# The q projection of two chunks as one Strassen pair, and a ring of weight sums at another place

## The chip, the cores and the metric

The kernel runs on one core of one Trainium2 chip. The core has five engines with instruction queues of their own: TensorE (PE in the profile, its weight loads PEld), VectorE (DVE), ScalarE (ACT), GpSimd (POOL) and SyncE (SP), which here only issues transfers. They work at the same time and meet at semaphores. The metric is the device time of one execution in microseconds; less is better. Before the change it is 770.33 us, the median of three runs (770.24 to 770.73).

## The reference

One transformer block over 2048 rows of 1024 values, in bfloat16. Its attention has 32 heads of 32 values and looks at eight earlier rows, two apart.

```python
qkv = (layernorm(x) @ wqkv)                      # 1024 -> 3 * 1024
idx = pos[:, None] - (jnp.arange(8) * 2)[None, :]
logits = einsum("bhsd,bhswd->bhsw", q, k[:, :, idx]) * 32 ** -0.5   # masked where idx < 0
o = einsum("bhsw,bhswd->bhsd", softmax(logits), v[:, :, idx])
h = x + o.reshape(B, S, D) @ wo
n = layernorm(h)
out = h + ((n @ w_gate) * (n @ w_up)) @ w_down   # 1024 -> 3584 -> 1024
```

## The kernel before, in words

The 2048 rows are four chunks (0 to 3) of 512. A chunk goes through normalization, q, k and v projection, attention, output projection `wo` with the residual, a second normalization, gate and up projections, their product, and the down projection.

**TensorE.** A product of a 128-column block of weights with a chunk is a group of eight 128x128 by 128x512 matmuls (`mm_group`, L431), each group into one of eight PSUM buffers. ScalarE copies most of them out (`evac_qkv`, L344; L717 and L724 for chunk 0's gate and up, L766 for chunk 1's). The weights stream through `wpool`, seven buffers of 1 MB (tag "w"): `pump` loads the next when fewer than seven are live, `retire` gives one back. wqkv has six blocks of 512 columns: 0 and 1 give q, 2 and 3 k, 4 and 5 v. One group is 1.73 us (`GROUP_US`).

**The order.** Each engine executes its instructions in the order in which the program issues them (`manual_schedule`). The order at the end of the function reads, for chunk and blocks: `qkv(0, 1..3)`, `qkv(1, 0..3)`, `qkv(0, 4..5)`, `qkv(1, 4..5)`, `qkv(2, 0..5)`, `qkv(3, 0..3)`, output projection 0 (`wo_ln2`), `qkv(3, 4..5)`, `ffn1_first` (gate and up of chunk 0, with output projection 1 in its middle, `wo_1`), `ffn1_second` (gate and up of chunk 1), `wo_adds(2)` (output projection 2). Then come the down projection of chunks 0 and 1 (lines `ex`, `ev`, `ey`, `ez`), output projection 3 in its middle, the gate and up projections of chunks 2 and 3 (`pair_block`), and their down projection (`dx`, `dy`). These last three are already computed by Strassen's scheme: seven products in place of eight over 2x2 blocks, with sums of blocks ahead and sums of results behind.

**Background work.** Attention of a chunk runs on VectorE: eight multiplications of 4096 elements per partition for the scores and eight for the values, with adds between, some 84 us a chunk. It is a Python generator. `Background` issues a piece of it after each group: `step` adds the group's time times `rate` to a credit of at most 4 us, and pieces are issued as long as the credit is positive, each taking the estimate that it yields. Other VectorE work is taken off with `spend`. A piece that yields `("later", us)` waits so long in the program's own count of time. So credit decides where in each queue an attention piece stands; it does not know how far an engine really is. Chunk 3's attention is cut off from the background at `wo_adds(2)`; its remaining pieces are issued by hand there and in the down projection (`pull`). The exp of each attention is on ScalarE (L499), the subtraction ahead of it (L497) on VectorE. An attention ends with its store and the loads of `oT` by GpSimd (L536, L539), which the output projection of the chunk needs.

**Sums for the scales.** The Strassen parts run in float16. Their weights are scaled by a power of two from the sum of absolute values. `Scale.add` sums one tile on ScalarE (L635), `rows` adds the columns up on VectorE (L639, L640), and `total` sums over the partitions by a product with ones on TensorE (L645), followed by five tiny VectorE steps (L647 to L654). For the down weights `abs_down` streams one half (columns 512 to 1023) in seven pieces through one `wpool` buffer, the ring, two pieces in flight; the other half is summed by `abs_blocks` at the start of `wo_adds(2)`, sixteen ScalarE passes (`junkb`). `scale_d.rows()` and `scale_d.total()` stand in the first products of the down projection.

Of the kernel before, what the change touches and what calls it, by code (L numbers as in the profile page):

```python
# [78 lines left out]
def kernel(  # L79
# [46 lines left out]


# [72 lines left out]
    def load_x(c, what, eng):  # L200
        tiles = []
        for t in range(4):
            xt = hp.tile([128, D], BF, tag="h", name=f"{what}{c}_{t}")
            eng.dma_start(xt[:], x[bass.ds(c * TC + t * 128, 128), :])
            tiles.append(xt)
        return tiles
# [52 lines left out]
    class NormOnScalar(Norm1):  # L259
# [16 lines left out]
        def devs(self):  # L276
            nc.scalar.activation(self.nm, self.s, ACTF.Copy, scale=-1.0 / D)
            for t in range(4):
                nc.scalar.activation(self.junk[:], self.xs[t][:], ACTF.Square, bias=self.nm[:, t:t + 1],
                                     accum_out=self.ss[:, t:t + 1])  # L280
                yield "later", self.pace
            nc.scalar.activation(self.rs4[:], self.ss, ACTF.Ln, bias=eps[:], scale=1.0 / D)
            nc.scalar.activation(self.rs4[:], self.rs4[:], ACTF.Exp, scale=-0.5)
            for t in range(4):
                nc.scalar.activation(self.nb[:, t:t + 1], self.nm[:, t:t + 1], ACTF.Copy, scale=self.rs4[:, t:t + 1])
# [14 lines left out]
        def rows(self):  # L300
            for t in range(4):
                self.row(t)
                self.transpose(t)
                yield "later", self.pace

# [33 lines left out]

    qkv_in = {}  # L340

    def evac_qkv(c, m, ps):
        sg = t1k.tile([128, HB + TC], BF, tag="t1k", name=f"sg{c}_{m}")
        nc.scalar.copy(sg[:, HB:HB + TC], ps[:])  # L344
        hg = m % 8
        if m >= 8:
            nc.scalar.copy(sg[:, 0:HB], halo[:, m - 8, :])
            if c + 1 < NCH:
                nc.scalar.copy(halo[:, m - 8, :], ps[:, TC - HB:TC])
        if m < 8:  # L350
            nc.sync.dma_start(qd[c][:, 4 * hg:4 * hg + 4, :, :].rearrange("c g d s -> (g d) c s"),
                              sg[:, HB:HB + TC].rearrange("p (c s) -> p c s", c=4))
            return
        dst = (kd, vd)[m // 8 - 1][c]
        base = sg[:, 0:1]
        win = bass.AP(base.tensor, base.offset, [list(base.ap[0]), [SUB, 4], [1, SUB + HB]])
        nc.sync.dma_start(dst[:, 4 * hg:4 * hg + 4, :, :].rearrange("c g d s -> (g d) c s"), win)
# [76 lines left out]
    def qkv(c, blocks, last=False):  # L434
        for b in blocks:
            for j in range(4):
                ps = psum.tile([128, TC], F32, tag="mm", name=f"ps{c}_{b}_{j}")
                mm_group(ps, wts["qkv", b], j, lnTs[c])
                evac_qkv(c, b * 4 + j, ps)
                bg.step(GROUP_US)  # L440
            if last:
                retire()
# [5 lines left out]
    def load_qk(c):  # L448
        qD = att.tile([128, DH, SUB], BF, tag="qD", name=f"qD{c}")
        kD = att.tile([128, DH, SUB + HB], BF, tag="kD", name=f"kD{c}")  # L450
        nc.gpsimd.dma_start(qD[:], qd[c].rearrange("c g d s -> (c g) d s"))
        nc.gpsimd.dma_start(kD[:], kd[c].rearrange("c g d s -> (c g) d s"))
        qkv_in["q", c], qkv_in["k", c] = qD, kD
# [14 lines left out]
    def attention(c):  # L468
        while c and c - 1 not in over:
            yield "later", 1.0  # L470
# [71 lines left out]
        while c + 1 < NCH and ("q", c + 1) not in qkv_in:  # L542
            yield "later", 1.0
            prefetch_qk(c + 1)
        if c + 1 < NCH:
# [4 lines left out]
    class Norm2(NormOnScalar):  # L550
# [11 lines left out]
        def finish(self):  # L562
            yield from self.devs()
            yield from self.rows()
# [4 lines left out]
    def wo_norm(c):  # L569
# [4 lines left out]
        for t in range(4):  # L574
            for hf in range(2):
# [6 lines left out]
                if hf == 0 and t > 0:  # L582
                    n.sum(t - 1)
                bg.step(GROUP_US)
        n.sum(3)
        retire(2)
        return n

    def wo_ln2(c, at={}):
        lnT = lnTp.tile([128, KO, TC], BF, tag="lnT", name=f"lnT2_{c}")  # L590
        hs = hss[c]
        mv4, rs4 = ln_tiles(f"2_{c}")

        def norm(t):
            ln = normalize(hs[t], mv4, rs4, t)
            nc.sync.dma_start_transpose(lnT[:, :, bass.ts(t, 128)], ln[:])

        for t in range(4):
            for hf in range(2):
                ps = psum.tile([128, 512], F32, tag="mm", name=f"wo{c}_{hf}_{t}")  # L600
                for kk in range(KO):
                    nc.tensor.matmul(ps[:], lhsT=oTs[c][:, kk, t, :], rhs=wts["wo", c, hf][:, kk, :],
                                     start=(kk == 0), stop=(kk == KO - 1))
                nc.vector.tensor_tensor(hs[t][:, bass.ts(hf, 512)], ps[:], hs[t][:, bass.ts(hf, 512)], ALU.add)
                if hf == 1:
                    stats(hs[t], mv4, t)
                    rstd_of(mv4, rs4, t, t + 1)
                    bg.spend(1.5)
                elif t > 0:
                    norm(t - 1)  # L610
                    bg.spend(0.55)
                bg.spend(0.7)
                if 2 * t + hf in at:
                    at[2 * t + hf]()
                bg.step(GROUP_US)
        norm(3)
        retire(2)
        for t in range(4):
            rows = hsd[c][:, t, :]
            nc.sync.dma_start(rows, hs[t][:, D - rows.shape[-1]:D])  # L620
        return lnT, hs

    ones = const.tile([128, 128], BF)
    nc.vector.memset(ones[:], 1.0)

    class Scale:
        def __init__(self, name, n):
            self.name, self.n = name, n  # L630
            self.l1 = const.tile([128, n], F32, name="l1" + name)
            self.rowb = const.tile([128, 1], BF, name="rowb" + name)

        def add(self, k, src, junk):
            nc.scalar.activation(junk, src, ACTF.Abs, accum_out=self.l1[:, k:k + 1])  # L635

        def rows(self):
            row = small.tile([128, 1], F32, tag="l1row", name="row" + self.name)
            nc.vector.tensor_reduce(row[:], self.l1[:], mybir.AxisListType.X, ALU.add)  # L639
            nc.vector.tensor_copy(self.rowb[:], row[:])  # L640

        def total(self, ps=None):
            n = TC if ps else 64
            ps = ps or psum.tile([128, TC], F32, tag="mm", name="l1ps" + self.name)
            nc.tensor.matmul(ps[:, 0:n], lhsT=ones[:], rhs=self.rowb[:].to_broadcast((128, n)), start=True, stop=True)  # L645
            tot = const.tile([128, 1], F32, name="tot" + self.name)
            nc.vector.tensor_copy(tot[:], ps[:, 0:1])  # L647
            eb = const.tile([128, 1], I32, name="eb" + self.name)
            nc.vector.tensor_scalar(eb[:], tot[:].bitcast(I32), 0x7F800000, None, ALU.bitwise_and)
            nc.vector.tensor_scalar(eb[:], eb[:], float(27 << 23), None, ALU.max)  # L650
            sb = const.tile([128, 1], I32, name="sb" + self.name)
            nc.vector.tensor_scalar(sb[:], eb[:], -1.0, float(266 << 23), ALU.mult, ALU.add)
            ib = const.tile([128, 1], I32, name="ib" + self.name)
            nc.vector.tensor_scalar(ib[:], eb[:], float(12 << 23), None, ALU.subtract)  # L654
            self.s, self.inv = sb[:].bitcast(F32), ib[:].bitcast(F32)
# [8 lines left out]
    def abs_down():  # L664
# [11 lines left out]
        for p in range(7):  # L676
# [3 lines left out]
            yield "later", 4.9 * GROUP_US  # L680
# [193 lines left out]

    qkv(0, range(1, 4))
    load_qk(0)
    bg.finish(rows2)
    for t in range(4):
        norm1[2].transpose(t)
    xtiles[3] = load_x(3, "x", nc.sync)  # L880
    pump(6)
    state["live"] += 1
    bg.add(norm1[3].sums(), bg.now + 18.0)
    start_attention(0)
    sums = abs_down()
    bg.add(sums, bg.now + 25.0, first=True)
    qkv(1, range(4))
    qkv(0, range(4, 6))
    load_v(0)
    bg.add(norm1[3].rows(), bg.now, first=True)  # L890
# [3 lines left out]
    qkv(2, range(6))  # L894
    start_attention(2)
    hss[0] = load_x(0, "h", nc.sync)
    qkv(3, range(4), last=True)
    bg.finish(atts[0])
    bg.rate = 1.03
    bg.spend(8.0)  # L900
    nxt = wo_ln2(0)
    qkv(3, range(4, 6), last=True)
# [3 lines left out]
    def wo_1():  # L906
        bg.finish(sums)
# [6 lines left out]
    hT0 = ffn1_first(nxt[0], {(4, 2): wo_1})  # L914
    bg.finish(norm2[1])
    ffn1_second(norm2[0].lnT, {})

    def f16(ap):
        return ap.bitcast(F16)
# [137 lines left out]
    def total_h1():  # L1057
# [3 lines left out]
                4: in_turn(total_h1, lambda: pull(1)), 6: lambda: pull(1)})  # L1061
# [292 lines left out]
```

## Time and profile before

The times are microseconds from the start of the profiled execution, whose span is 768.7 us.

| stage | TensorE, us | what else is at work |
|---|---|---|
| first rows, q of chunk 0 | 0 to 17.7 | loads, normalization of chunk 0 |
| q, k, v of chunks 0 to 3 (block 3 of chunk 3 last) | 17.7 to 163.6 | attention 0 on VectorE, 52.3 to 136.6 |
| output projection 0 | 163.6 to 177.4 | attention 1 stands still for adds and statistics |
| v of chunk 3 | 177.4 to 191.2 | attention 1 |
| gate and up of chunk 0, output projection 1 within | 191.2 to 301.7 | attention 1 to 237.1, then attention 2 |
| gate and up of chunk 1 | 301.7 to 398.4 | attention 2 to 333, then attention 3 |
| output projection 2 | 398.4 to 412.6 | sixteen `junkb` passes on ScalarE |
| down projection of chunks 0 and 1, output projection 3 | 412.6 to 511 | rest of attention 3 |
| gate and up of chunks 2 and 3, down projection | 511 to 768 | Strassen sums on GpSimd, VectorE and ScalarE |

A line of the chain in order of time has the start, the time and the work, with its line in the code. A line of a timeline has the start, the duration, the engine, the line, the operation, output and inputs with their shape, and how many were merged; in brackets stands how long the engine was idle before it and what it waited for. A duration counts from the start of the instruction, so two that follow one another may overlap by a little. The ring's seven passes on ScalarE take 1.91 us each.

### The profile page before, as it was taken

The page shows a single profiled execution, that of the slowest core. Times are in us where ns is not written, and L with a number is a line of the kernel's source. Part 1 is how long each engine was busy: PE and PEld are TensorE (multiplying, and loading weights), DVE is VectorE, ACT ScalarE, POOL GpSimd, SP SyncE. Part 2 cuts the span into 40 slices and gives each one's busy share as a digit, 9 for nine tenths or more (in the row PEclk, how much of TensorE's full clock was granted, in tenths as well). Part 3 has the DMA queues.
Part 4 walks back from the last instruction along what each step waited for, and adds up shares of the span by engine and source line. Part 5 has one row for each costly group of instructions (what it writes and reads, how often), then busy time and mean ns, then how long its engine had stood idle before and what let it go on. Part 6 is the DMA issues. An engine that isn't in the chain of part 4 may idle for free.

```text
span 768.7 us, 10302 instructions
## 1 busy us (share of the span) xinstructions
PE 762.8 (99%) x3663; PEld 350.7 (46%) x3663; DVE 606.0 (79%) x718; ACT 513.1 (67%) x979; POOL 142.5 (19%) x152
## 2 busy tenths in 40 slices
PE   8999999999999999999999999999999999999998
PEld 5444444444444444444444444444444444444444
DVE  5639999999999999999998997975454444568863
ACT  4648966423687398778899986736777677788240
POOL 0000000200002000020000001018778677600000
PEclk9999999999999999999999999999999999999999
DMA  8999796999966699579559448674342423730001
GB/s 268 272 257 260 207 269 153 279 305 283 301 219 216 210 299 294 172 246 326 194 186 300 139 155 279 126 198 107 80 110 55 110 74 91 257 126 29 0 29 55
DMA packets 190915, 144.85 MB, mean 188 GB/s; under 512 B 81808, under 2 KB 181136, under 8 KB 188688
## 3 DMA queue, kind: packets, MB, share of 16 engines
q1 hardware_dynamic: 180416, 116.94, 54.2%
q0 software_dynamic: 3584, 22.02, 8.4%
q10 hardware_dynamic: 6864, 5.24, 2.5%
q8 instruction: 28, 0.46, 0.2%
q14 instruction: 23, 0.19, 0.1%
HBM read 110.10 MB, written 27.26 MB: 179 GB/s over the span
## 4 chain that ended last, share of the span: by engine, by line
PE 97%; DVE 2%; DMA 1%; issue 0%; ACTq 0%; DVEq 0%
PE ps L431 21%; PE dx L944 6%; PE pz L826 6%; PE pwu L431 6%; PE pu L431 6%; PE py L826 6%; PE pwg L431 6%; PE pg L431 6%; PE px L826 6%; PE wo L998 4%; PE pv L826 3%; PE ez L944 3%; PE ey L944 3%; PE ex L944 3%; PE dy L944 3%; PE wo L578 2%
## 5 line engine op out<-in xcount | busy, mean ns | idle before, releaser
L431 PE MATMUL ps<-lnT,w_qkv 128*128 128x512 bf16 x736 | 159.5, 379 | 0.0
L431 PEld LDWEIGHTS <-w_qkv 128*128 128x128 bf16 x736 | 71.9, 98 | 86.1 <-issue 0.2
L344 ACT CAST sg<-ps 128x512 bf16<-128x512 f32 x96 | 55.2, 586 | 46.9 <-PE ps L431 41.6
L477 DVE TENSOR_TENSOR prod<-qD,kD 128x4096 bf16<-128x4096 bf16 x32 | 72.2, 2284 | 12.8 <-DMA kD<-kd 12.8
L523 DVE TENSOR_TENSOR pv<-vD,at 128x4096 bf16<-128x4096 bf16 x32 | 72.4, 2285 | 0.2
L826 PEld LDWEIGHTS <-sw 128*128 128x128 f16 x448 | 43.8, 98 | 52.9 <-issue 0.2
L431 PEld LDWEIGHTS <-w_wu 128*128 128x128 bf16 x448 | 43.8, 98 | 52.9
L431 PEld LDWEIGHTS <-w_wg 128*128 128x128 bf16 x448 | 43.8, 98 | 52.9
L826 PE MATMUL px<-lnT,ws 128*128 128x512 bf16 x224 | 55.2, 379 | 0.0
L536 POOL DMA_DIRECT2D od<-oD x4 | 2.2, 544 | 275.6 <-DVE oD L534 275.6
L431 PE MATMUL pg<-lnT,w_wg 128*128 128x512 bf16 x224 | 52.9, 379 | 0.0
L431 PE MATMUL pu<-lnT,w_wu 128*128 128x512 bf16 x224 | 52.9, 379 | 0.0
L431 PE MATMUL pwu<-lnT,w_wu 128*128 128x512 bf16 x224 | 52.9, 379 | 0.0
L431 PE MATMUL pwg<-lnT,w_wg 128*128 128x512 bf16 x224 | 52.9, 379 | 0.0
L826 PEld LDWEIGHTS <-ws 128*128 128x128 f16 x336 | 32.9, 98 | 39.6
L807 POOL TENSOR_TENSOR sw<-ws 128x512 f16<-128x512 f16 x26 | 30.0, 1155 | 82.4 <-PE pv L826 49.1
L944 PEld LDWEIGHTS <-gs 128*128 128x128 f16 (+1 forms) x280 | 27.4, 98 | 33.0
L479 DVE TENSOR_TENSOR prod<-prod 128x4096 bf16<-128x4096 bf16 x16 | 36.6, 2288 | 0.4
L843 ACT COPY py<-px 128x512 f32<-128x512 f32 x28 | 16.0, 570 | 27.7 <-PE px L826 27.7
L808 POOL TENSOR_TENSOR sw<-sw,ws 128x512 f16<-128x512 f16 x26 | 30.0, 1154 | 2.0
L810 POOL TENSOR_TENSOR sw<-ws,sw 128x512 f16<-128x512 f16 x26 | 30.3, 1167 | 0.0
L809 POOL TENSOR_TENSOR sw<-ws 128x512 f16<-128x512 f16 x26 | 30.1, 1156 | 0.0
(334 smaller groups left out, 1472.9 us busy)
## 6 DMA issues: line engine op xcount, KB each, us to landing
w_wg<-in_B_w_gate_dram SPq DMA_DIRECT2D x14, 1024.0 KB, 6.9
w_wu<-in_B_w_up_dram SPq DMA_DIRECT2D x14, 1024.0 KB, 6.3
w_pair<-in_B_w_gate_dram SPq DMA_DIRECT2D x14, 512.0 KB, 4.0
w_pair<-in_B_w_up_dram SPq DMA_DIRECT2D x14, 512.0 KB, 5.3
w_wo<-in_A_wo_dram SPq DMA_DIRECT2D x6, 1024.0 KB, 7.6
w_qkv<-in_A_wqkv_dram SPq DMA_DIRECT2D x5, 1024.0 KB, 11.5
kd<-sg SPq DMA_DIRECT2D x32, 144.0 KB, 4.4
kD<-kd POOLq DMA_DIRECT2D x4, 1152.0 KB, 8.6
```

The costliest lines, as they stand in the source:

```text
L344: nc.scalar.copy(sg[:, HB:HB + TC], ps[:])
L431: nc.tensor.matmul(ps[:], lhsT=wt[:, ko, bass.ts(j, 128)], rhs=rhs[:, ko, :], start=(ko == 0), stop=(ko == KO - 1))
L477: nc.vector.tensor_tensor(prod[:, j], qD[:], kD[:, :, o:o + SUB], ALU.mult)
L479: nc.vector.tensor_tensor(prod[:, :, 0:16], prod[:, :, 0:16], prod[:, :, 16:32], ALU.add)
L523: nc.vector.tensor_tensor(pv[:, j], vD[:, :, o:o + SUB], at[:, w, None, :].to_broadcast((128, DH, SUB)), ALU.mult)
L807: eng.tensor_tensor(sw[:, i, 0], a21, a22, ALU.add)
L808: eng.tensor_tensor(sw[:, i, 1], sw[:, i, 0], a11, ALU.subtract)
L809: eng.tensor_tensor(sw[:, i, 2], a11, a21, ALU.subtract)
L810: eng.tensor_tensor(sw[:, i, 3], a12, sw[:, i, 1], ALU.subtract)
L826: nc.tensor.matmul(ps[:], lhsT=lhs[:, ko, :], rhs=rhs[:, ko, :], start=(fresh and ko == 0), stop=(ko == 3), skip_group_check=not fresh)
L944: nc.tensor.matmul(ps[:, bass.ds(lo, n)], lhsT=lhs[k][:, bass.ts(q, 128)], rhs=rhs[k][:, bass.ds(lo, n)], start=(fresh and k == 0), stop=( ...
L998: nc.tensor.matmul(ps[:], lhsT=oTs[c][:, kk, t, :], rhs=wts["wo", 2, hf][:, kk, :], start=(kk == 0), stop=(kk == KO - 1))
```

## The change

**The q projection of chunks 2 and 3.** Blocks 0 and 1 of wqkv, for both chunks, are taken out of `qkv(2, ...)` and `qkv(3, ...)` and computed by two calls of `q_pair`, each for two of four column blocks: seven products of four matmuls instead of eight. For this:

- `scale_q` sums the absolute values of blocks 0 and 1 while chunk 0 is projected (two parts on VectorE, two on ScalarE); `q_convert` then turns both blocks into scaled float16 in place, and chunk 1's q is computed from these and scaled back.
- `q_weight_sums` (sixteen VectorE sums) runs in the background before attention 0, and its results stay in eight `t1k` buffers and four of `hp`.
- `q_row_sums` (twelve sums) follows attention 0, into twelve `t1k` buffers; `q_last_sum` makes the last one, t3, in a new `wpool` buffer `room_q`. Attention 1 is held back until t3 is issued.
- `q_pair(0)` stands ahead of output projection 0, `q_pair(2)` behind it and between the groups of chunk 3's block 5. In each, ScalarE makes six copies between PSUM buffers, four stagings and two parts p5, VectorE four evictions with a sum.

**Output projection 0.** `wo_ln2`, with its statistics and normalization on VectorE, goes. `wo_norm(0, devs=False)` does sums and squares on ScalarE and the four normalized rows on VectorE. The rate of the background becomes 1.06 in place of 1.03.

**The ring of row sums of the down weights.** `abs_down` moves from chunk 1's q, k and v projections, where a piece came every 4.9 groups, to `ffn1_second`, one every 7.

**Small moves.** The loads of chunk 0's q and k, and of chunk 3's x, stand behind earlier transfers; chunk 3's first normalization comes earlier as one piece; `wo_1` comes two groups later; `total_h1` in `wo_adds(2)` moves from step 4 to step 6.

```diff
+    def q_row_sums():
+        while 0 not in over:
+            yield "later", 0.5
...
+        for k in range(4):
+            nc.vector.tensor_tensor(t1[k], b12[:, k, :], b11[:, k, :], ALU.subtract)
+            nc.vector.tensor_tensor(t2[k], b22[:, k, :], t1[k], ALU.subtract)
...
+    def q_last_sum(room):
+        t3 = room[:, 2:4, :].rearrange("p a c -> p (a c)").bitcast(F16).rearrange("p (k c) -> p k c", k=4)
+        nc.vector.tensor_tensor(t3, lnTs[3][:, 4:8, :], lnTs[3][:, 0:4, :], ALU.subtract)
+        qsum["t3"] = [t3[:, k, :] for k in range(4)]
...
     def attention(c):
-        while c and c - 1 not in over:
+        while c and (c - 1 not in over or c == 1 and "t3" not in qsum):
             yield "later", 1.0
...
-            yield "later", 4.9 * GROUP_US
+            yield "later", 7.0 * GROUP_US
...
-    qkv(2, range(6))
+    qkv(2, range(2, 6))
+    rows_q = q_row_sums()
+    bg.add(rows_q, bg.now, first=True)
+    qkv(3, [2, 3], last=True)
+    hss[0] = load_x(0, "h", nc.sync)
+    state["live"] += 1
+    qkv(3, [4], last=True)
+    bg.finish(atts[0])
+    bg.finish(rows_q)
+    room_q = wpool.tile([128, 4, TC], F32, tag="w", name="room_q")
+    q_last_sum(room_q)
+    bg.spend(bg.credit)
+    bg.rate = 1.06
+    q_pair(0, room_q)
+    bg.spend(1.0)
+    norm2 = [wo_norm(0, devs=False)]
+    norm2.append(norm2[0].finish(devs=False))
+    bg.add(norm2[1], bg.now, first=True)
+    qkv(3, [5], js=(0, 1))
+    q_pair(2, room_q, between=(lambda: qkv(3, [5], js=(2,)), lambda: qkv(3, [5], last=True, js=(3,))))
+    bg.finish(norm2[1])
+    retire(3)
...
-    qkv(3, range(4), last=True)
-    bg.finish(atts[0])
-    bg.rate = 1.03
-    bg.spend(8.0)
-    nxt = wo_ln2(0)
-    qkv(3, range(4, 6), last=True)
...
-    hT0 = ffn1_first(nxt[0], {(4, 2): wo_1})
+    hT0 = ffn1_first(lnT2_0, {(4, 3): wo_1})
     bg.finish(norm2[1])
+    state["live"] += 1
+    sums = abs_down()
+    bg.add(sums, bg.now, first=True)
     ffn1_second(norm2[0].lnT, {})
+    bg.finish(sums)
...
-                4: in_turn(total_h1, lambda: pull(1)), 6: lambda: pull(1)})
+                4: lambda: pull(1), 6: in_turn(total_h1, lambda: pull(1))})
```

## The prediction

> **What bounds the kernel now.** First the page: busy shares, the 40 slices, the chain that ended last.
>
> ```profile
> PE 762.8 (99%) x3663; PEld 350.7 (46%) x3663; DVE 606.0 (79%) x718; ACT 513.1 (67%) x979; POOL 142.5 (19%) x152
> PE   8999999999999999999999999999999999999998
> DVE  5639999999999999999998997975454444568863
> ACT  4648966423687398778899986736777677788240
> PE 97%; DVE 2%; DMA 1%; issue 0%; ACTq 0%; DVEq 0%
> ```
>
> TensorE is the bound: it fills every slice after the first. But VectorE is also full from slice 4 to slice 20 (58 to 400 us), with the four attentions. Taking work from TensorE helps only while VectorE and ScalarE keep up with it. So next the chain in order of time, for the place where TensorE first needs a late product of both.
>
> ```profile
> 163.61 13.81 PE wo L602 x64
> 398.44 8.63 PE wo L998 x40
> 412.57 9.06 PE ex L944 x42
> 421.64 0.21 PE ey L645
> ```
>
> L645 at 421.64 us is the ones-matrix product of `scale_d.total`: TensorE multiplies a vector that VectorE made (L639, L640) from sums that ScalarE made (L635). Products execute in order, so all later ones queue behind it. The timelines of the two engines show how near they are there.
>
> ```profile
> 136.59 4.49 DVE L477 TENSOR_TENSOR prod<-qD,kD 128x4096 bf16<-128x4096 bf16 x2
> ...
> 172.30 1.28 DVE L604 TENSOR_TENSOR h<-wo,h 128x512 bf16<-128x512 f32 x2
> ...
> 185.62 2.28 DVE L479 TENSOR_TENSOR prod<-prod 128x4096 bf16<-128x4096 bf16 x1
> ```
>
> ```profile
> 380.17 1.23 DVE L497 TENSOR_TENSOR lg<-lg,mx 128x1024 f32<-128x1024 f32 x1
> ...
> 418.86 0.18 DVE L639 TENSOR_REDUCE rowd<-l1d 128x1 f32<-128x23 f32 x1 [0.43 <-ACT junkb L635]
> ...
> 421.89 0.16 DVE L647 COPY totd<-ey 128x1 f32<-128x1 f32 x1 [1.46 <-PE ey L645]
> ```
>
> ```profile
> 381.43 1.06 ACT L499 ACTIVATE lg<-lg 128x1024 f32<-128x1024 f32 x1 [3.72 <-DVE lg L497]
> ...
> 418.63 0.19 ACT L635 ACTIVATION_READ_ACCUMULATOR junkb<-w_dn 128x1 f32 x1
> ```
>
> Three things to see. Chunk 1's attention starts on VectorE at 136.59, right behind chunk 0's. ScalarE, in order, stands 3.72 us at chunk 3's exp (L499), because VectorE has only just finished the subtraction at 381.40. And from there to 418.82 ScalarE works without a gap over 0.2 us: 22.16 busy of 22.38 us from 381.43 to 403.81, 15.01 of 15.01 to 418.82 (busy time by stretch). The vector for L645 is ready at 419.2, TensorE comes for it at 421.64: 2.4 us of slack in the whole chain VectorE, exp, ScalarE, L639, L645.
>
> **What the Trainium skill says.** "TensorE: Matmul & The Clock Gate", section Back-to-back issue gap: 518 cycles for 512 columns, some 216 ns; a group of eight takes 1.727 us here, 215.9 ns each, which agrees. "PSUM — Partial Sum Buffer", section Engine vs sequencer instructions: the queues of ScalarE and VectorE are strict FIFO and matmuls keep program order; the 3.72 us with evictions queued behind the exp agree. "VectorE: DVE Perf Modes", section The perf-mode tier table: 16-bit `tensor_tensor` runs at 2x, 1224 ns for 2048 elements; L481 shows 1.222 us.
>
> **The change, part by part.**
>
> *TensorE.* Sixteen groups of eight (8 of chunk 2, 8 of chunk 3) become two pairs of 2 x 7 products of 4: 128 matmuls become 112. Sixteen times 0.2158 us is 3.45 us; the 64-column sum of `scale_q` costs back about 0.1. Alone this gives 770.33 - 3.35 = 767.0.
>
> *Chunk 0.* VectorE gains two absolute reductions of 2048 elements (not in the trace: 1.22 us at L481's rate, 2.3 at the 1x rate of the tier table; I take 2.1), two conversions (L802: 1.28) and 16 sums (L1112: 0.415 each), 4.2 + 2.6 + 6.6 = 13.4 us; ScalarE gains two passes of 1.91 us. Before its first product at 52.34 VectorE waited 12.77 us for kD, and 4 us for rstd values, so this is hidden. kD comes about as before, as the x load now stands behind it: I count attention 0 as ending at 136.6, as now.
>
> *Row sums and the wait for t3.* Twelve sums of 0.415 us follow attention 0: 5.0 us, to 141.6. Then `q_last_sum` writes into `room_q`, from the seven-buffer weight pool. Six are held there (q blocks 0 and 1, block 5, wo twice, the first gate block), so it gets the buffer of block 4, free when TensorE ends chunk 3's block 4: 163.61 less 16 groups plus 4, 163.61 - 20.72 = 142.9, with the sum 143.0. The sum t3 takes 1.22 us (2048 elements): done at 144.3. Attention 1 is held until t3 is issued, so it starts 7.7 us later than at 136.59. Queued behind it on VectorE is everything to L645.
>
> *VectorE from there to the exp of chunk 3.* Removed: statistics, normalization and adds of `wo_ln2`, 172.30 to 185.62, 13.3 us. Added: 8 evictions of the pairs and 8 adds, back to back 0.60 to 0.62 us as L784 and L1000 are (0.75 where they wait), and 4 rows (L192, 0.47): 11.8. Idle that a later VectorE wins back: 0.97 and 1.56 (gs waiting for ScalarE) and 0.57 (wo of chunk 1), 3.1. Sum: 7.7 - 13.3 + 11.8 - 3.1 = +3.1, so the subtraction ends at 384.5. With every wait before 381 won back and no other loss it is +1.8; with slower evictions and full exp waits +6.
>
> *How much attention is issued.* The yields of one attention are 82.9 us of credit. The new rate 1.06 over 252 us gives 267; the spends (evictions 6, adds 10, gs 10, products 8.7, the rest 7) take 42. That leaves 225, as many as are issued now at 1.03: at the end of `ffn1_second` chunk 3 has again two scores' worth of its 15 value steps behind it (six), and the exp again stands some 22 us before that end. So no attention is moved past it; VectorE is simply asked for more than it can do.
>
> *The ring of absolute sums.* Seven passes of 1.91 + 0.19 us leave chunk 1's projections and go into the second gate and up stage, first after 12 us, then every 12.1, on a ScalarE that is busy 62.45 of 77.70 us from 300 to 377.70. The first five fit its idle 15 us and the wait at the exp. The last two come about 16 and 2 us before the stage's end, behind the exp, where nothing is idle: +4.2 us.
>
> *Sum.* The last `junkb` ends at 418.82 + 3.1 + 4.2 = 426.1, the vector at 426.5. TensorE would be there at 421.64 - 3.35 = 418.3 and waits. L645 comes 4.9 us later than now; its slack of 2.4 is already used in that. After it 347 us of TensorE work follow, unchanged and without waits: 770.33 + 4.9 = **775.2 us**. The bounds of VectorE's term, +1.8 and +6, give 773.9 and 778.1.
>
> *Output projection 1.* It moves two groups later, so to the same 253.4 us. Its oT is issued at 244.34, once attention 1 ends at 237.1. With attention 1 ending 5.2 us later (7.7 - 1.5 of the exchange - 1.0 of idle) and 3.7 to 8.1 us to land, TensorE waits 0 to 4 us there. This comes out of the lead that L645 takes anyway, so it costs nothing more. `total_h1` from step 4 to 6 of output projection 2 gives that product 3.45 us; L645 stays where it is.
>
> **The rivals.**
>
> *All is hidden: 767.0.* For: TensorE shows no wait after 9 us, and the slack of eight PSUM buffers is 14 us of groups. Against: L645 would have to come at 418.3, so VectorE's subtraction at about 377, 7 us before my sum.
>
> *It comes out even: 770.5.* If ScalarE reaches the exp late but takes its two passes in gaps, only VectorE counts: its own path to L639 had 2.4 + 0.43 us of slack, and +3.1 uses it up: L645 at 421.9. Against: the full 22.16 of 22.38 us.
>
> *More stalls: 782.* Of 30 buffers of `t1k`, the sums hold 20 through the pairs, leaving 10 for staging q, k and v; and a ScalarE that stands 8 us at the exp lets TensorE fill all eight PSUM buffers. Each may cost 3 us more. For: SyncE's queue is backed up there. Against: ten buffers are 17 us of groups, the stores land in 4.
>
> **How the numbers follow.** The chain through the exp 0.55, within 772 to 779; hidden 0.22; even 0.13; more stalls 0.10. The hidden case is over the 2 in 10 that may be left out, so the range takes it in: 766.8 to 779.5. Bounds of no change are 768.8 and 771.9: faster 0.23, same 0.14, slower 0.63.
>
> **What would show it.** Chunk 1's first product on VectorE at about 144 rather than 136.6, after a wait at t3. A longer ScalarE wait at chunk 3's exp (7 us or so). TensorE idle before L645, with L639 still ended by ScalarE's `junkb`. Two ring passes between the exp and `junkb`. I am wrong if chunk 3's subtraction ends before 379 us, or if TensorE shows no idle from 395 to 425.

## The result, and the profile after

The changed kernel takes 774.5 us (median of four runs, 774.2 to 774.72), the kernel before beside it 770.38 us (770.24 to 770.73): a ratio of 1.0053, 95% interval 1.0035 to 1.007. It is slower by 4.1 us; 775.2 was predicted.

The page of the changed kernel: first the busy times, then three rows of the slices, then the shares of the chain that ended last.

```profile
PE 758.6 (98%) x3592; PEld 349.4 (45%) x3648; DVE 623.4 (81%) x754; ACT 532.2 (69%) x1009; POOL 144.3 (19%) x154
PE   8999999999999999999997999999999999999998
DVE  6779999899999999999998997985553444578863
ACT  4756964565777397798999985835777677788240
PE 78%; DVE 9%; ACT 7%; issue 3%; DMA 2%; ACTq 0%; DVEq 0%
```

TensorE has less to do (758.6 us in place of 762.8), yet it has a hole: the 7 in the 22nd slice, 406 to 425 us. The chain is no longer 97% TensorE. From 351 to 424 us it runs over a transfer and ScalarE. TensorE's timeline there:

```profile
410.18 0.39 PE L378 MATMUL l1psh<-rowbh,ones 128*128 128x512 bf16 x1 [1.18 <-DVE rowbh L373]
410.40 1.89 PE L1147 MATMUL wo<-w_wo,oT 128*128 128x512 bf16 x7
412.13 9.23 PE L1093 MATMUL ex<-w_dn,gs 128*128 128x512 bf16 x42
424.18 0.59 PE L378 MATMUL ey<-rowbd,ones 128*128 128x512 bf16 x1 [2.82 <-DVE rowbd L373]
425.41 14.89 PE L1093 MATMUL ex<-w_dn,gs 128*128 128x512 bf16 x63 [0.22 <-issue]
```

L378 is the old L645. `l1psh` is the product of the same kind for `scale_h1`, in output projection 2. The product `ey` waits 2.82 us for the vector of `scale_d`, as predicted. The matmul behind the wait takes 0.59 us and not 0.38: the granted clock has dropped. Spans differ by +4.2 us (772.9 against 768.7). That is -3.35 for the saved matmuls, +1.8 for three early waits (0.81 at `qy`, a product of the pair; 0.30 at `pg`, the first gate group; 0.67 at output projection 1), +1.18 and +2.82 for the two waits above, and some +1.7 for the lower clock and the gap behind. The clock term belongs to the traced execution alone: the other three kept a mean clock of 1.000 and still have spans of 772.4 to 772.8. What fills that time in them is not shown.

VectorE around t3, and its timeline at chunk 3's subtraction (L559, before: L497) and at the vector:

```profile
142.57 1.23 DVE L945 TENSOR_TENSOR room_q<-lnT 128x2048 f16<-128x2048 bf16 x1 [1.65 <-PE ps L488]
143.72 4.49 DVE L539 TENSOR_TENSOR prod<-qD,kD 128x4096 bf16<-128x4096 bf16 x2
...
383.76 1.23 DVE L559 TENSOR_TENSOR lg<-lg,mx 128x1024 f32<-128x1024 f32 x1
...
423.76 0.18 DVE L372 TENSOR_REDUCE rowd<-l1d 128x1 f32<-128x23 f32 x1 [2.16 <-ACT junkb L368]
```

ScalarE's timeline from 362 us on; L561 is the exp of chunk 3 (before: L499), `w_ring` a pass of the ring:

```profile
362.34 0.59 ACT L778 CAST ring<-pwg 128x512 bf16<-128x512 f32 x1 [2.46 <-DMA hd<-ring]
...
385.06 1.08 ACT L561 ACTIVATE lg<-lg 128x1024 f32<-128x1024 f32 x1
...
389.90 1.94 ACT L368 ACTIVATE w_ring<-w_ring 128x2048 bf16<-128x2048 bf16 x1
...
401.46 2.02 ACT L368 ACTIVATE w_ring<-w_ring 128x2048 bf16<-128x2048 bf16 x1
...
423.54 0.19 ACT L368 ACTIVATION_READ_ACCUMULATOR junkb<-w_dn 128x1 f32 x1
```

Two passes stand behind the exp, as predicted. But at the exp there is no wait: ScalarE itself is as late as VectorE (385.06 against 384.99). From 362.34 to the exp it has no gap over 0.45 us, so the fifth pass, at 373.45, went into no idle time. One reason more stands in the first line. ScalarE waited 2.46 us at an eviction (below: the stand at hd), because the buffer it writes (a tile of `ffn1_second` that is also named `ring`; the ring of weight sums is `w_ring`) was still being stored to `hd`. In the chain that store reads:

```profile
351.11 11.15 DMA hd<-ring
```

11.15 us from issue to landing; the median of all transfers of `hd` is 5.3. Most of this is not new. In the kernel before, the store of that place was issued at 349.7:

```profile
DMA to landing us min/median/max: 9.9/9.9/9.9
```

So in the changed kernel it is issued 1.4 us later, behind a later VectorE, and then takes 1.25 us more.

### The profile page after: what moved, and what is told of

It reads as the page before. It is cut to its first block, busy times and chain, and to the rows that moved or that the text cites. A ratio compares the mean times of both kernels' runs of the same rounds, so it can differ in the third digit from the quotient of the medians.

```text
span 772.9 us, 10278 instructions
## 1 busy us (share of the span) xinstructions
PE 758.6 (98%) x3592; PEld 349.4 (45%) x3648; DVE 623.4 (81%) x754; ACT 532.2 (69%) x1009; POOL 144.3 (19%) x154
## 4 chain that ended last, share of the span: by engine, by line
PE 78%; DVE 9%; ACT 7%; issue 3%; DMA 2%; ACTq 0%; DVEq 0%
PE ps L488 16%; PE dx L1093 6%; PE pz L838 6%; PE pu L488 6%; PE pg L488 6%; PE py L838 6%; PE px L838 6%; ACT ring L368 3%; PE pv L838 3%; PE ez L1093 3%; PE ey L1093 3%; PE dy L1093 3%; PE wo L655 2%; PE ex L1093 2%; DVE prod L539 2%
## 5 line engine op out<-in xcount | busy, mean ns | idle before, releaser
L488 PE MATMUL ps<-lnT,w_qkv 128*128 128x512 bf16 x595 | 131.6, 379 | 0.7
L488 PEld LDWEIGHTS <-w_qkv 128*128 128x128 bf16 (+1 forms) x608 | 59.3, 98 | 70.9
L402 ACT CAST sg<-ps 128x512 bf16<-128x512 f32 x72 | 41.6, 584 | 31.8 <-PE ps L488 27.2
L838 PE MATMUL px<-lnT,ws 128*128 128x512 bf16 x212 | 53.1, 379 | 0.6
```

The lines of the kernel that those rows point to most:

```text
L488: nc.tensor.matmul(ps[:], lhsT=wt[:, ko, bass.ts(j, 128)], rhs=rhs[:, ko, :], start=(ko == 0), stop=(ko == KO - 1))
L838: nc.tensor.matmul(ps[:], lhsT=lhs[:, ko, :], rhs=rhs[:, ko, :], start=(fresh and ko == 0), stop=(ko == 3), skip_group_check=not fresh)
```

## The experiments

**The theories.** A, from the prediction: two loads on one chain (VectorE, exp, ScalarE, L378), the held-back attention and the ring's passes. B: early waits and buffers of the pairs. C1, C2: the ring alone, or the q pair alone. After the first four runs a theory S was added: ScalarE's own queue, filled by the ring's passes and by what the ring's buffer and transfers cause, sets the end. All ratios are to runs of the kernel before on the same chip, with the 95% interval.

| kernel | us, median | ratio |
|---|---|---|
| before + ring moved | 782.78 | 1.0155 (1.014 to 1.017) |
| before + ring's passes moved, no loads, no buffer | 776.89 | 1.0083 (1.0069 to 1.0097) |
| after | 774.5 | 1.0053 (1.0035 to 1.007) |
| after, ring back in q, k, v | 782.36 | 1.0146 (1.0112 to 1.018) |
| after, ring left out | 770.06 | 0.9992 (0.9984 to 1.0001) |
| after, ring's passes only | 772.45 | 1.0025 (1.0015 to 1.0036) |
| after, ring a stage earlier | 777.24 | 1.0083 (1.007 to 1.0097) |

**Ring only, on the kernel before.** `abs_down` goes to the second gate and up stage, at the pace of the change; nothing else.

```diff
-            yield "later", 4.9 * GROUP_US
+            yield "later", 7.0 * GROUP_US
...
+    state["live"] += 1
+    sums = abs_down()
+    bg.add(sums, bg.now, first=True)
     ffn1_second(norm2[0].lnT, {})
+    bg.finish(sums)
```

> The kernel before, with only the ring of absolute sums moved to the gate and up stage of chunk 1 (one piece per 7 groups); no q pair. Theory A (two loads on one chain, VectorE to exp to ScalarE to L645: the ring's two late passes behind chunk 3's exp cost +4.2 us there, the held-back attention 1 another 3 us or so): the exp stays at about 381.4, the last junkb pass ends at 421 to 423 instead of 418.8, TensorE waits 1 to 3 us at the ones product of scale_d; 771.5 to 773.5 us. Rival C1 (the ring alone accounts for the loss and the q pair hides its own): at least as late as the changed kernel relative to its ideal, 776 to 778 us, since the 3.4 us gain is missing. Rival C2 (the ring is harmless, all comes from the q pair): 770.0 to 770.8 us and no wait before the ones product.

It took 782.78 us, later than every theory had it. From the waits of TensorE, and ScalarE's timeline:

```profile
PE l1psh L645 <- ACT junkb L635: 7.4, 1, 7.4
```

```profile
368.39 0.58 ACT L766 CAST ring<-pwg 128x512 bf16<-128x512 f32 x1 [7.26 <-DMA hd<-ring]
...
388.71 1.09 ACT L499 ACTIVATE lg<-lg 128x1024 f32<-128x1024 f32 x1
```

The same stand at a store, here 7.26 us: the store was issued at 352.98 and landed 15.33 us later. ScalarE reaches the exp at 388.71 (before: 381.43), VectorE waits behind it in turn, and the product of `scale_h1` (`l1psh`), still at step 4 of output projection 2, waits 7.4 us. So the ring's move costs far more than its passes, and the move of `total_h1` to step 6 is part of what it needs.

**Ring's passes only, on the kernel before.** The same, but the seven passes read a weight tile that is there anyway.

```diff
-        ring = wpool.tile([128, KO, 512], BF, tag="w", name="w_ring")
...
-            scale_d.add(p, rows_of(p), rows_of(p))
-            if p + 2 < 7:
-                load(p + 2)
+            scale_d.add(p, state["src"][:, 0:4, :], state["junk"])
```

> The kernel before with the ring's seven ScalarE passes in chunk 1's gate and up stage, over a weight tile that is there anyway: no loads of the ring, no buffer held (seven sums are those of other weights). Beside the kernel before with the whole ring moved, which took 782.8 us, it tells how much of those 12 us is the buffer. If the buffer made ScalarE's 7.3 us stand at hd: the stand is under 2 us and the time 771.5 to 775 us. If the passes alone fill ScalarE's queue: 779 us or more. The total of scale_h1 stands at step 4 here and may wait up to 4 us.

776.89 us, 5.9 less than with loads and buffer, but 1.9 over its range. The stand at hd is 0.3 us. ScalarE's exp, and the one wait of TensorE after its start:

```profile
381.19 1.06 ACT L499 ACTIVATE lg<-lg 128x1024 f32<-128x1024 f32 x1 [1.57 <-DVE lg L497]
```

```profile
410.68 0.39 PE L645 MATMUL l1psh<-rowbh,ones 128*128 128x512 bf16 x1 [3.85 <-ACT junkb L635]
```

The exp stays (381.19), the wait at it shrinks from 3.72 to 1.57: the five earlier passes go into idle time, this wait among it. The last `junkb` ends at 422.50 in place of 418.82, +3.68, for two passes behind the exp. That is the prediction's term for the ring (+4.2), alone and a little smaller. The wait of 3.85 at `l1psh` and a clock of 0.83 over 10 us (1.7 us) make 5.6 us, all of the 5.3 by which the traced execution is longer than the kernel before (774.0 against 768.7). It is the fastest of five; the others, with a mean clock of 0.995 in place of 0.998, took 776.55 to 777.46.

**Ring left out.** The changed kernel without `abs_down`; its seven columns are 0.

```diff
-    state["live"] += 1
-    sums = abs_down()
-    bg.add(sums, bg.now, first=True)
     ffn1_second(norm2[0].lnT, {})
-    bg.finish(sums)
...
+    nc.gpsimd.memset(scale_d.l1[:, 0:7], 0.0)
```

> The changed kernel without the ring: its seven loads, seven ScalarE passes and its weight-pool buffer are left out (its seven sums are taken as 0). Theory S, formed after the first four runs (ScalarE's own queue sets the ones product of scale_d: the ring's passes of 2.1 us and the 2.5 us stand at a store of hd, which the missing buffer causes, and VectorE's subtraction at 384.95 only happens to be ready at the same time): ScalarE reaches chunk 3's exp early and waits there for VectorE, which still ends the subtraction at about 384.9; two passes fewer stand behind the exp, the last junkb ends at about 419.5 instead of 423.7; TensorE waits 0 to 0.5 us at the ones product, the waits before 260 us (1.8) stay; 768.8 to 770.2 us. Theory A (VectorE, held back by the row sums, sets it alone): the wait stays over 2 us, 773 us or more. Rival B (the early waits): 772 us or more.

770.06 us, within S's range and below A's. The exp on ScalarE, then L378 on TensorE:

```profile
383.96 1.06 ACT L561 ACTIVATE lg<-lg 128x1024 f32<-128x1024 f32 x1 [3.82 <-DVE lg L559]
```

```profile
420.79 0.38 PE L378 MATMUL ey<-rowbd,ones 128*128 128x512 bf16 x1
```

Now VectorE sets the exp, 2.53 us later than before, and L378 still follows without a wait. It is close: the vector is ready at 420.62, and TensorE comes at 420.79 only because it lost 2.38 us on the way. So a later VectorE costs nothing here, but it would if the early waits were gone. With the ring gone the change is even (0.9992). The difference to the whole change is the ring, about 4.5 us. Of the 3.35 us saved, those 2.38 go at once (0.82 at `qy`, 0.34 at `pg`, 1.22 at oT of output projection 1); some 0.7 more are spread over the rest, and where was not found.

**Ring's passes only, on the changed kernel.** The edit is that of the passes on the kernel before.

> The changed kernel with the ring's seven ScalarE passes kept, but over a weight tile that is there anyway: no loads of the ring and no weight-pool buffer held (seven sums are those of other weights). It parts ScalarE's time from the buffer and the transfers. If the buffer matters (with six buffers the weight loads wait in SyncE's queue, and the stores of hd behind them hold up ScalarE's evictions): the 2.5 us stand of ScalarE at hd goes, the last junkb ends 1 to 2.5 us earlier, 771.5 to 773.5 us. If only the passes matter: 774 to 775 us. If the transfers alone matter: 768.8 to 770.2 us, as without the ring.

772.45 us, as expected if the buffer and the transfers matter. ScalarE's exp and TensorE's L378:

```profile
383.73 1.06 ACT L561 ACTIVATE lg<-lg 128x1024 f32<-128x1024 f32 x1 [0.82 <-DVE lg L559]
```

```profile
422.94 0.38 PE L378 MATMUL ey<-rowbd,ones 128*128 128x512 bf16 x1 [2.23 <-DVE rowbd L373]
```

The stand at hd is gone, and the exp waits for VectorE again: this is the chain as the prediction drew it, VectorE late by 2.3 us and two passes behind the exp, 2.23 us at L378. So the passes cost 2.4 us against the version without the ring, loads and buffer 2 us more (the halved clock of its traced execution included, which this run doesn't have). Where these act is seen at the store of `hd`. In the four kernels without the ring's loads there (before, passes only on either kernel, ring left out) it is issued at 349.5 to 350.1, takes 9.6 to 10.0 us and lands at 359.5 to 359.8. In the changed kernel it lands at 362.26, with the whole ring on the kernel before at 368.31. The DMA share between 360 and 370 us goes along: 0.56 to 0.66 in the four, 1.01 and 1.08 in the two with the ring; from 350 to 360 it is 0.97 to 1.05 in all six. But the share alone proves little: with the ring a stage earlier it is 1.01 too, and without the ring, output projection 1 later, 1.03. That the ring's loads lengthen a stretch with full DMA engines fits; buffer and loads were not parted from one another.

**Stores of hd from GpSimd.**

```diff
-            nc.sync.dma_start(hd1[:, bass.ts(i, 2), :], g)
+            nc.gpsimd.dma_start(hd1[:, bass.ts(i, 2), :], g)
```

> The changed kernel with one edit: the stores of chunk 1's products (hd) are issued by GpSimd instead of SyncE, so that they no longer stand behind weight loads that wait for a buffer. Theory S: ScalarE's 2.5 us stand at hd goes, ScalarE reaches the exp of chunk 3 sooner and then waits up to 2.5 us for VectorE, so part of the gain is lost there; the last junkb ends 0 to 2.5 us earlier, 772.0 to 774.5 us. If the order in SyncE's queue has no part in it: 774.5 us and the same stand.

781.12 us (ratio 1.0137, 1.0116 to 1.0158): a miss. The chain of waits names the store:

```profile
349.58 12.49 DMA hd<-ring
```

In GpSimd's queue it stood behind the loads of oT, before which GpSimd was idle for 6.38 us. Issued at 349.58, 1.5 us ahead of SyncE's in the changed kernel, it landed at 362.07, when that one did (362.26). ScalarE reached the buffer earlier and stood 9.21 us. So the queue that issues the store doesn't decide when it lands; the traffic between 350 and 362 us does, as far as these runs can tell.

**Ring back in the q, k and v stage.**

```diff
-            yield "later", 7.0 * GROUP_US
+            yield "later", 4.9 * GROUP_US
...
+    state["live"] += 1
+    sums = abs_down()
+    bg.add(sums, bg.now + 18.0, first=True)
     for t in range(4):
```

> The changed kernel with the ring put back to the q, k and v stage of the first chunks (one piece per 4.9 groups); its buffer then serves as room_q. Theory A: the subtraction of chunk 3 still ends at 384 to 385, but two passes fewer stand behind the exp, so the vector of the ones product is ready 4 us earlier, at 420: TensorE waits 0 to 1 us there instead of 2.8, the early waits (1.8 us) stay; 769.5 to 771 us. Rival C1 (the ring alone): all waits from 400 on are gone, 767.0 to 768.5 us. Rival C2 (the q pair alone, ring harmless): the wait stays at 2.8 us, 774 to 775 us. Rival B (the early waits of the pairs and of output projection 1 carry the loss): 774 to 775 us as well, but with the 2.8 us wait gone.

782.36 us, outside every range, and widely spread: six executions from 775.9 to 785.96. The 775.9 is the only one whose mean clock stayed at 1.000; the trace is of the 784.29, with the clock halved for 10.24 us. The late part behaves as A had it (the wait at `ey` is 0.4 us), but the early part breaks:

```profile
PE ps L488 <- ACT halo L407: 11.0, 3, 7.9
```

```profile
ACT sg L402 <- DMA vd<-sg: 10.8, 1, 10.8
```

ScalarE stands 10.8 us at a staging buffer (`t1k`) whose store has not landed, and TensorE behind it 11.0. The weight sums hold eight of these buffers from before attention 0 on. The first pass came at 89.9 us here and at 80.6 in the kernel before, so it isn't the old place to the group. With the ring in that stage this stand is there, and without it (the changed kernel) it isn't. That the eight buffers are what is missing is likely but was not tested: SyncE was also held 7.71 us at a transposing load ahead of the stores. In the kernel before it was held 11.09 us at one, and ScalarE didn't stand. If it is the buffers, the ring's move belongs to the q pair.

**Row sums on GpSimd; and the same with the ring back.** The twelve sums and t3 go to GpSimd as soon as their inputs are there, and attention 1 isn't held back.

```diff
-            nc.vector.tensor_tensor(t1[k], b12[:, k, :], b11[:, k, :], ALU.subtract)
-            nc.vector.tensor_tensor(t2[k], b22[:, k, :], t1[k], ALU.subtract)
+            nc.gpsimd.tensor_tensor(t1[k], b12[:, k, :], b11[:, k, :], ALU.subtract)
+            nc.gpsimd.tensor_tensor(t2[k], b22[:, k, :], t1[k], ALU.subtract)
```

> The changed kernel with the twelve row sums and t3 on GpSimd in place of VectorE, made as soon as the chunks' normalized columns are there; room_q takes the buffer of an earlier block, so attention 1 follows attention 0 without being held back. The ring stays in chunk 1's gate and up stage. Theory A: attention 1 starts 6 to 7 us earlier (136 to 138), the subtraction of chunk 3 ends 3 to 4 us earlier (381 to 382), the ring's passes behind the exp stay: the wait before the ones product falls from 2.8 us to 0 to 1.5; 771 to 773 us. Rival C1 (the ring alone sets it, the held-back attention is made up by idle won back): no change, 774 to 775 us. Rival C2 (the held-back attention alone): all of it, 767.5 to 769 us.

> Both remedies together: the row sums and t3 on GpSimd with attention 1 not held back, and the ring back in the q, k and v stage of the first chunks. Theory A: the two costs add up on one chain, so with both gone no wait is left before the ones product, and only the small waits of the pairs (0.8) remain: 767 to 769 us, faster than the kernel before. Rival B (early waits, PSUM and staging buffers of the pairs carry the loss): 772 us or more, with waits between 142 and 260 us. Rival D (the clock or the issue of TensorE is lower with the pairs themselves): above 770 us without any named wait.

803.36 and 804.14 us (ratios 1.0426, 1.0413 to 1.044, and 1.0448, 1.0429 to 1.0466). Neither tests A, because GpSimd isn't free. Timelines of the two engines in the first of them:

```profile
118.75 3.13 DVE L596 TENSOR_TENSOR oD<-oD,pv 128x4096 bf16<-128x4096 bf16 x1
```

```profile
113.49 3.08 POOL L929 TENSOR_TENSOR qt<-lnT,qt 128x512 f16<-128x512 bf16 x1
```

VectorE's 4096-element operations take 3.13 us beside GpSimd's and 2.28 alone; GpSimd's 128x512 sums take 3.1, where later ones of the same size take 1.15. And beside t3, GpSimd's one long sum:

```profile
144.04 6.03 DVE L596 TENSOR_TENSOR oD<-oD,pv 128x4096 bf16<-128x4096 bf16 x1
```

```profile
141.82 6.10 POOL L940 TENSOR_TENSOR room_q<-lnT 128x2048 f16<-128x2048 bf16 x1
```

Attention 0 ends at 150 us, not 136, the pair's evictions stand behind it, and TensorE waits 10.0 us in output projection 0 alone. "SBUF — State Buffer" of the Trainium skill, section SBUF: two separate sides, says that VectorE and GpSimd share a port pair under an exclusive lock. The trace fits such taking of turns: from 106 to 128 us each of the two starts one operation every 3.16 us, and beside t3 VectorE's operation is longer by 3.75 us. The trace doesn't part waiting from work within an operation.

**Row sums left out, attention 1 not held back.**

```diff
-        qsum["b"] = (cells(b11), cells(b21), t1, t2, t4, cells(b22))
+        qsum["b"] = (cells(b11), cells(b21), cells(b12), cells(b22), cells(b21), cells(b22))
+        qsum["t3"] = cells(b22)
```

> The changed kernel without the twelve row sums and t3: the pairs multiply the chunks' normalized columns as they are (q of chunks 2 and 3 comes out as other numbers), and attention 1 isn't held back. The ring stays where it is. Theory A: VectorE's subtraction ends 4 to 7 us earlier (378 to 381), the wait before the ones product falls from 2.8 to 0 to 1 us; 770.5 to 772.5 us. Theory S: ScalarE does not wait for VectorE at the exp anyway, the last junkb stays at 423 to 424, 773.5 to 775 us. Rival B (staging buffers: twelve fewer are held): the waits before 260 us go, 772.5 us.

788.55 us (ratio 1.0233, 1.0218 to 1.0247): less work on VectorE, and much slower. The first eviction of the pair on VectorE in this kernel; before its number is compared, the wait that TensorE has at the first gate group:

```profile
157.43 0.74 DVE L968 SCALAR_TENSOR_TENSOR sg<-qz,ibq,room_q 128x512 bf16<-128x512 f32 x1
```

```profile
PE pg L488 <- DMA qd<-sg: 8.2, 1, 8.2
```

In the changed kernel that eviction starts at 151.71. Here attention 1 starts at 136.56, so 7 us more of it are in VectorE's queue ahead of the pair. The eviction comes 5.7 us later, SyncE stands at its store (15.12 us for eight stores, 9.96 in the changed kernel), and the normalized columns for the gates start 7.2 us later. Holding attention 1 back is not only a cost: it keeps the pairs' evictions at the front. The run can't tell what a less loaded VectorE would be worth, since it loses most of its time before 210 us.

**Ring a stage earlier.** Its passes go into chunk 0's gate and up stage, with `room_q`'s buffer.

```diff
-    retire(3)
+    retire(2)
+    sums = abs_down()
+    bg.add(sums, bg.now, first=True)
...
     hT0 = ffn1_first(lnT2_0, {(4, 3): wo_1})
+    bg.finish(sums)
```

> The changed kernel with the ring one stage earlier: its seven passes go into chunk 0's gate and up stage, where ScalarE is busy 12 of 20 us instead of 9.5 of 10, one per 7 groups, with the weight-pool buffer that room_q gives back. Theory S2 (the ring costs what its place makes it cost: ScalarE's passes behind chunk 3's exp, and a buffer less while ScalarE is full): no pass is left behind the exp, the stand at hd goes, ScalarE waits over 2 us for VectorE at the exp, no wait before the ones product of scale_d; 769.5 to 771.0 us, as without the ring. If seven passes and a buffer cost the same anywhere: 773.5 to 775 us. If chunk 0's stage is as tight (its weight loads behind a full pool): over 775 us, with waits of TensorE between 190 and 300 us.

777.24 us. No pass is behind the exp, and yet it is slower, by a wait that grew in that stage:

```profile
259.21 6.05 PE L655 MATMUL wo<-w_wo,oT 128*128 128x512 bf16 x21 [4.29 <-DMA oT<-od]
```

The store of attention 1 leaves at 245.46 (without the ring at 243.00), and the oT loads wait 8.00 us for it to land, not 5.66. VectorE is later and so is the landing; that the ring's transfers slow the latter here too was not shown by itself. The stand at hd, which was to go, is 3.66 us, with no transfer of the ring near it: the store took 9.8 us, but was issued as late as 357.19.

**Output projection 1 later.** With the ring a stage earlier, and without the ring:

```diff
-    hT0 = ffn1_first(lnT2_0, {(4, 3): wo_1})
+    hT0 = ffn1_first(lnT2_0, {(5, 0): wo_1})
```

> The ring in chunk 0's gate and up stage, and output projection 1 two groups later, so that oT of chunk 1 has landed. If the last wait before 260 us is only oT: 1.2 us less than with the ring's move alone, 768.3 to 769.8 us. If another wait takes its place (the normalized rows of chunk 1 for the second gate and up stage, two groups later too): the same time as with the ring's move alone.

> Without the ring (its loads, passes and buffer left out, its seven sums taken as 0), and output projection 1 two groups later. Against the version without the ring alone (770.06 us): if oT's 1.2 us pass through to the end, 768.7 to 769.2 us; if VectorE's lateness (the vector of the ones product is ready only as TensorE comes) takes them back there, 769.8 to 770.2 us and a wait of about 1 us at the ones product of scale_d.

779.04 and 775.29 us; each trace is of the slowest execution, 780.98 and 776.2 (ratios 1.0115, 1.0101 to 1.0128, and 1.0059, 1.0047 to 1.0072). The wait for oT goes, and another takes its place: the second gate and up stage waits for chunk 1's normalized columns, 9.71 and here 4.93 us.

```profile
304.49 3.60 PE L488 MATMUL pwg<-lnT,w_wg 128*128 128x512 bf16 x8 [4.93 <-DMA lnT<-ln]
```

The eight matmuls behind it take 3.60 us in place of 1.89. Two groups later is no better place for output projection 1. No run was clearly faster than the kernel before.

## Why the prediction was right

**TensorE, -3.35: right.** The first gate group starts at 188.71 us in place of 191.07; that is 2.4 us earlier with 1.1 us of waits ahead of it.

**Chunk 0 hidden: right.** Attention 0 ends at 136.1 us (136.6 predicted).

**t3 and the held-back attention: right.** Sums done at 140.9 (141.6), TensorE frees block 4 at 142.5 (143.0), attention 1 starts 7.1 us later (7.7). That it is nothing but a delay was wrong: without it the pairs' evictions come late.

**Subtraction of chunk 3 at 384.5: right.** 384.99; 383.93 without the ring and 383.69 with its passes only, so the ring's loads and buffer add a microsecond to VectorE too.

**Two passes behind the exp, +4.2: right, 0.4 too large.** They start at 389.90 and 401.46, and the next eviction 1.89 and 1.91 us later: the 0.19 us for reading the sum, which the prediction added, overlaps. Alone, on the kernel before, the two make +3.68.

**A 7 us wait of ScalarE at the exp: wrong.** There was none. The prediction moved VectorE by 3.1 us and left ScalarE at its place ahead of the exp. But ScalarE was ready for the exp, which is its start less its wait, at 377.71 before, at 380.15 without the ring, at 382.91 with its passes only and at 385.06 in the change. So of 7.35 us some 2.4 come without the ring (their cause is open), 2.8 from passes that the prediction put into idle time and into this very wait, and 2.15 from the ring's loads and buffer, which it left out; they lengthen the stand at hd from 0.8 us without the ring to 2.46. This step hardly moved the sum, as VectorE was ready only 0.1 us before ScalarE.

**Last `junkb` at 426.1: 2.4 us too late.** It ends at 423.73. From the exp to there it was 38.67 us, not 41.6: the two passes take 3.8 and not 4.2, and with the exp later, one weight pass and one eviction less (some 2.4 us) stood behind it.

**TensorE at L378 at 418.3, waits from then on as one: mis-sized.** It came at 421.36, since 1.8 us of early waits and 1.18 at `l1psh` were already spent. The prediction had the early waits as coming out of this lead, and so it was. The wait was 2.8 us, not 8.

**347 us behind it unchanged: wrong by 1.5 us** in the traced execution, for the clock. There the sum of 775.2 holds a delay that was 2.3 us too large (L378 at 424.18 against 426.5) and lacks that term and the gap behind. That the two nearly cancel is luck. So is the distance of 0.7 us to the median: the other three executions, without a lower clock, came to 774.2 to 774.58 by a sum that no trace shows. What was predicted and is shown is the chain: VectorE late at the exp, two passes behind it, a wait at L378.

**The rivals.** "All is hidden" falls with the result, and even without the ring it is 770.06, not 767. "Even" (770.5) is what the change would be without the ring. "More stalls" did not come true in the change, but nearly every edit of its placement brought one.

## What to carry to other kernels

Cost a moved stream by its transfers and its buffer as well as by its passes: look at the DMA share of the stretch it moves into, and at when the stores whose buffers are written next are issued and land. A kernel whose places are tuned against each other has slack of one or two groups on both sides of a step (here oT ahead of output projection 1, normalized columns behind it), so a saving in one stage is often spent at the next wait. And an operation that is held back may be what keeps a short urgent one at the front of an in-order queue.

## What the runs showed of the hardware

A wait of TensorE can cost more than its length, and where it falls decides. In all fourteen traces the granted clock is either full or half, and changes only on a grid of 3.41 us: each stretch at half clock begins a whole multiple of 3.41 us after the first record of the clock and lasts 3.41 us or a multiple of it (up to 17.07), if the end of the program doesn't cut it. Rows by stretch, cut on this grid; the first column of busy time is TensorE's, the column ahead of the DMA share and GB/s the granted clock. After, wait of 2.82 us from 421.36:

```profile
420.42:423.83 3.41, 0.94 (x5) 0.30 (x4) 1.25 (x2) 3.41 (x9) 0.00 (x0) 1.00 1.04 332
423.83:427.24 3.41, 2.84 (x7) 1.14 (x8) 3.24 (x10) 3.41 (x3) 0.00 (x0) 0.50 0.06 20
```

Stores of hd from GpSimd, a wait of 2.17 us from 397.44, and one of 2.81 us from 428.51:

```profile
396.31:399.72 3.41, 1.24 (x7) 0.49 (x5) 3.38 (x3) 3.41 (x6) 0.00 (x0) 1.00 0.33 110
399.72:403.13 3.41, 3.41 (x9) 1.18 (x8) 3.41 (x3) 3.41 (x5) 0.54 (x1) 0.50 0.46 159
...
427.03:430.44 3.41, 1.48 (x7) 0.59 (x6) 1.72 (x2) 3.41 (x9) 0.00 (x0) 1.00 1.10 348
430.44:433.85 3.41, 2.48 (x11) 1.17 (x12) 2.78 (x10) 3.41 (x4) 0.00 (x0) 1.00 1.08 344
```

The wait of 2.17 us lies in one stretch and halves the clock of the next; that of 2.81 us is split over two and doesn't. Over all traces, each stretch at full clock in which TensorE was busy for 1.28 us or less is followed by half clock (16 of them), and none in which it was busy for 1.33 us or more. So a wait is punished when it takes more than some 2.1 us of one stretch. Half speed for one stretch is at most 1.7 us of work lost. A tail of a long wait can keep the clock down for another stretch: behind the wait of 4.93 us of the last run it is half for 6.83 us.

"TensorE: Matmul & The Clock Gate", section What's actually happening, says that the clock halves after an idle window of about 3.4 us, that a busy one restores it, and that the windows run freely. Half clock, window and free grid agree. That the window must be idle doesn't: in the two above TensorE worked for 0.94 and 1.24 us, and the clock fell. As the grid isn't at a fixed place to the program (its first record lies 4.0 to 7.2 us behind the start), a wait between about 2.1 and 4.2 us (twice 2.1, when two stretches share it) should be costed with a chance of up to 1.7 us more, and a longer one with that cost.
